# Filler matmuls in TensorE's waits, and a second pass that runs backwards: attention with two FFNs on one core

## The chip, the cores and the metric

The kernel runs on one core of a Trainium2 chip. The metric is the device time of one execution in microseconds (us); lower is better. Engines are named as in the profile: PE is TensorE (its weight loads are PEld), DVE is VectorE, ACT is ScalarE, POOL is GpSimd, SP is SyncE, whose queue issues the DMAs.

## The reference, cut to what matters

```python
batch, n_heads, seq, head_dim = (4, 8, 576, 64)      # q, k, v
n_tokens, d_model = 2304, 512                        # d_ff: 1024, then 2048

def _attn_ref(q, k, v):
    scores = scale * np.matmul(q, k.transpose(0, 1, 3, 2))
    mask = block_i >= block_j                        # blocks of 64 positions
    scores = np.where(mask, scores, -1000000000.0)
    scores = scores - np.max(scores, axis=-1, keepdims=True)
    attn = np.exp(scores)
    attn = attn / (np.sum(attn, axis=-1, keepdims=True) + 1e-09)
    return np.matmul(attn, v)

def _moe_ref(x, w_in, w_out, g_ln):                  # the first FFN
    h = x @ w_in
    e = np.exp(h - np.max(h, axis=-1, keepdims=True))
    solu = h * (e / (np.sum(e, axis=-1, keepdims=True) + 1e-09))
    mu, var = mean and variance of solu over its row
    return ((solu - mu) / np.sqrt(var + 1e-06) * g_ln) @ w_out

def _moe2_ref(x, w_in, w_out):                       # the second FFN
    h = x @ w_in
    return (h * (1.0 / (1.0 + np.exp(-1.702 * h)))) @ w_out
```

All is float32.

## The kernel before, in words

**Three stages share the engines.** Attention runs batch by batch (4 batches, 4 pairs of heads each). For a pair, `scores` multiplies queries by keys on PE, DVE takes the result out of PSUM with the block mask (tile `mask`, zeros but for one corner) and the row maximum (`mx`), ACT makes the exponentials (`P`, `PR`), PE transposes them against `ident` (`u_pt`), and PE multiplies by `v` (`u_pv`). The attention output goes to DRAM (`xd`) and comes back as tiles of 128 tokens (`x`, split into a high and a low part, `xs`) for the first FFN (`h_mm`, `solu_ln`, `ln_t`, `y_mm`). While batch 0 runs, the weights of the first FFN are converted as well (`w1_prep`, tiles `e`, `yo`, `junk`). The first FFN's output goes to DRAM (`y1d`).

**The second FFN** works on chunks of tokens, 640, 640, 512 and 512 of them, and on 8 pairs of weight blocks, `p` = 0 to 7, of which SBUF holds four at a time (`slots`). So it makes two passes over all chunks: pairs 0 to 3 for chunk 0, then chunks 1, 2, 3; then pairs 4 to 7 for chunks 0, 1, 2, 3. A step is one (pair, chunk). In a step `h2_steps` makes seven products (a Strassen-like scheme; tiles `p`, `u`, `hc`, `sg`, then `gH` and `gL`), and `out_steps` adds pair `p`'s part of the output into accumulators that PSUM holds for the chunk, one bank for each 128 tokens. At the end of the first pass over a chunk the accumulators are copied out and stored in DRAM (`part`); at the end of the second pass they are read back (into `land` and `wt`) and added. Before a chunk starts, `y_load` fetches its tokens (`x<-y1d`), `y_sums` makes four sums (tiles `t` and `x`), and `y_split` splits seven operands into high and low parts (tiles `w1i` and `xs`, whose first use is over by then). `prep_w2` makes a pair's weights from DRAM (`wt<-w2d`, then `stmp`, `w2A`, `w2B`, `w2S`, `w2o`), and runs for pairs 4 to 7 while the first pass is at its last chunk.

**The order of instructions** comes from a list scheduler, the class `Recorder`. Every operation is recorded with a priority, and `issue` emits them one by one to the engine on which they can start first, by the costs in `_cost`. Each engine has a time `free[e]` up to which the scheduler believes it busy, and `start` is when it believes the next operation can begin. For some copies and sums it may choose between two engines. PSUM is eight banks that it hands out itself (`bank_free`, `bank_t`). Since every instruction is emitted in `_emit`, all carry line L383 (L387 after the change), and tiles tell them apart. A change of `mode` (the shape of the weights that PE holds) costs 0.09 in the scheduler's account (`SWITCH`), so a matmul put in between can change what is chosen next.

Of the kernel before, what the change touches and what calls it, by code (L numbers as in the profile page):

```python
# [16 lines left out]
ALU = mybir.AluOpType  # L17
# [42 lines left out]
class Recorder:  # L60
# [6 lines left out]
    SPAN = 10  # L67
    OWN = 0.15
    LEAVE = (0, 1, 1)
    SWITCH = 0.09  # L70
    STAY = 0.0
    LOAD = {'vector': 2.0}
# [3 lines left out]
    def __init__(self, tc, banks):  # L76
        self.banks = banks
        self.n_bank = banks.shape[1]
        self.bank_free = [True] * self.n_bank
        self.bank_t = [0.0] * self.n_bank  # L80
        self.n_buf = 0
        self.places = {}

        self.floor = 0.0
        self.tc = tc
        self.nc = tc.nc
        self.prio = 0.0
        self.tag = None
        self.n_tag = {}
        self.open = None  # L90

        self.also = []
        self.ops = []
        self.tensors = {}
        self.free = dict.fromkeys(self.ENGINES, 0.0)
        self.port = 0.0
        self.dma = 0.0
        self.now = 0.0
        self.mode = None
        self.heap = {e: [] for e in self.ENGINES}  # L100
        self.log = []
        for e in self.ENGINES:
            setattr(self, e, _Engine(self, e))
# [281 lines left out]
    def _waiting(self):  # L385
# [5 lines left out]
        ]  # L391
        return min(late, default=1e9)

    def issue(self, tag=None):

        with self.tc.manual_schedule():
            while any(self.heap.values()) and (tag is None or self.n_tag.get(tag, 0)):
                best = None
                waiting = self._waiting()
                for e, heap in self.heap.items():  # L400


                    for prio, i in heap:
                        op = self.ops[i]
                        start = self._start(op, e)
                        if start < 1e9 and prio > waiting + self.YIELD and any(b.at is None for b in op.bufs):
                            start += 1e6
                        key = (start, prio + (self.STAY if self._switch(op, e) else 0.0), i)
# [9 lines left out]
                op = self.ops[i]  # L418
                if start >= 1e6:
                    start = self._start(op, e)  # L420
                for x in op.forms:
                    self.heap[x].remove((prio, i))
                prio = op.prio
                start += self._switch(op, e)
                if e == "tensor":
                    self.mode = op.mode
# [32 lines left out]
                for j in op.users:  # L459
                    o = self.ops[j]  # L460
# [15 lines left out]
def kernel(  # L476
# [19 lines left out]
    NT, DM = out.shape  # L496
# [119 lines left out]

    def clear():
        nc.vector.memset(mask, 0.0)
        nc.vector.memset(mask[0:64, 448:512], -1e30)
        for t in vb:  # L620
            nc.gpsimd.memset(t[64:128, KT - 1], 0.0)
        for x in Pb:
            nc.gpsimd.memset(x["R"][:, S:], 0.0)
        for t in qR:
            for x in t:
                nc.gpsimd.memset(full(x), 0.0)
# [478 lines left out]


    m2_p = ctx.enter_context(tc.tile_pool(name="m2", bufs=1, side="right", reuse_waits="tile"))
    sizes = [640, 640, 512, 512]
    chunks = [(sum(sizes[:i]), n) for i, n in enumerate(sizes)]
    CM = max(sizes)  # L1110
    HM = CM // 2
# [180 lines left out]
    def out_steps(cc, p):  # L1292
        c0, n = chunks[cc]
        g = gs.pop((cc, p))
        O = slots[p % NSLOT][3]
        first, last = p % NSLOT == 0, p % NSLOT == NSLOT - 1
        if first:
            acc[cc] = [nc.bank(0, name="acc") for _ in range(n // 128)]
            for a in acc[cc]:
                a.buf.held = True  # L1300
        if last and p >= NSLOT:
            pb = [pbs[next(n_pb) % len(pbs)] for _ in acc[cc]]
            for i, x in enumerate(pb):
                nc.sync.dma_start(out=x, in_=part[cc][i * 128:(i + 1) * 128])
        for i, a in enumerate(acc[cc]):
            sl = slice(i * 128, (i + 1) * 128)
            todo = [(g[e][x][:, sl], O[e][y], e) for e in range(2) for x, y in ((0, 0), (0, 1), (1, 0))]
            with nc.group():
                for j, (x, y, e) in enumerate(todo):
                    nc.tensor.matmul(a, lhsT=x, rhs=y, start=first and j == 0, stop=last and j == len(todo) - 1)  # L1310
            if last:
                a.buf.held = False

                at = obs + [x[:, 0:DM] for x in tmpb] if p == NPAIR - 1 and cc == len(chunks) - 1 else obs
                o = at[next(n_ob) % len(at)]
                if p < NSLOT:
                    nc.copy(o, a, "av")
                    nc.sync.dma_start(out=part[cc][sl], in_=o)
                else:
                    nc.vector.tensor_tensor(out=o, in0=a, in1=pb[i], op=ALU.add)  # L1320
                    nc.sync.dma_start(out=out[c0 + i * 128:c0 + (i + 1) * 128, :], in_=o)
            yield 6 * 0.231

# [28 lines left out]
    t = f_time  # L1352
# [2 lines left out]
        prep_w2(p)  # L1355
    nc.floor = 0.0
    went_ahead = []
    steps = [(h * NSLOT + p, cc) for h in range(2) for cc in range(len(chunks)) for p in range(NSLOT)]
    for n in range(len(steps) + 1):

        h2 = iter(())
# [7 lines left out]
        while its[0] or its[1]:  # L1369
# [5 lines left out]
                continue  # L1375
            went[i] += cost
            t += cost
        if n < len(steps) and p % NSLOT == NSLOT - 1 and n + 1 < len(steps):
            nc.prio = t + PY
            y_split(steps[n + 1][1])  # L1380
        if NSLOT <= n < NSLOT + 3 * (NPAIR - NSLOT) and n % 2 == 0 and len(went_ahead) < NPAIR - NSLOT:
# [4 lines left out]
        if n + 2 < len(steps) and p % NSLOT == 0:  # L1386

            nx = n + NSLOT
            if nx < len(steps):
                nc.prio = t  # L1390
                y_load(steps[nx][1])
                y_sums(steps[nx][1])
# [42 lines left out]
```

## Time and profile before

| | |
|---|---|
| three timed runs | median 783.81 us (782.36 to 786.83) |
| the profiled execution | 783.7 us |
| its span, first to last instruction | 781.9 us |
| instructions | 13917 |
| PE busy | 762.5 us (98%), 4936 matmuls |
| DVE, ACT, POOL busy | 539.4 us (69%), 442.0 us (57%), 290.8 us (37%) |
| granted TensorE clock, mean | 0.993 |

The busy time of PE has modelled ends, so a busy PE may still be a PE at half clock or with short gaps. What PE waited for, and what clock it was granted, have to be read from their own views. The second FFN begins at about 400 us, its second pass at about 592 us.

### The profile page before, as it was taken

To read this page: it belongs to the slowest core of one execution; us is meant where nothing else is said; L and a number is where in the kernel's file an instruction comes from. 1 tells how busy PE (TensorE), PEld (TensorE's weight loads), DVE (VectorE), ACT (ScalarE), POOL (GpSimd) and SP (SyncE) were. 2 spreads that over 40 slices of the span, in tenths; PEclk is the share of its full clock that TensorE was granted. 3 is DMA by queue.
4 is the path that set the end of the run, shared out by engine and by line. 5 is a ranking of instruction groups with operands and counts; after the bars stand their busy time and mean duration, and the time that the engine had idled before them with its cause. 6 is when DMAs were issued, how large, how long until landed. Compare 5 with 4: busy or idle time off the path is not lost.

```text
span 781.9 us, 13917 instructions
## 1 busy us (share of the span) xinstructions
PE 762.5 (98%) x4936; PEld 652.1 (83%) x4936; DVE 539.4 (69%) x1216; ACT 442.0 (57%) x1005; POOL 290.8 (37%) x365
## 2 busy tenths in 40 slices
PE   7999899999999999999999999999989899999998
PEld 4575586877887888989999998998989799999986
DVE  5978937656564558886748887867899875564644
ACT  6978767676585656565634654535565442433422
POOL 3544540142340264452231533344452253352422
PEclk9999799999999999999999999999999999999999
DMA  8976533442220245446502363455425123050201
GB/s 249 262 242 163 168 105 111 124 137 65 76 70 31 69 151 151 139 143 214 201 30 61 87 220 134 154 162 187 151 74 176 55 74 115 27 162 1 68 15 54
DMA packets 82342, 95.37 MB, mean 122 GB/s; under 512 B 11232, under 2 KB 57952, under 8 KB 82272
## 3 DMA queue, kind: packets, MB, share of 16 engines
q1 hardware_dynamic: 82128, 94.34, 38.6%
q8 instruction: 39, 0.64, 0.3%
q14 instruction: 31, 0.25, 0.1%
q10 hardware_dynamic: 144, 0.13, 0.0%
HBM read 69.21 MB, written 25.24 MB: 121 GB/s over the span
## 4 chain that ended last, share of the span: by engine, by line
PE 89%; DVE 5%; DMA 2%; ACT 1%; issue 1%; POOL 1%; SPq 0%; ACTq 0%; DVEq 0%; POOLq 0%
PE PS L383 89%; DMA xd<-xo 1%; DVE st L383 1%; DMA x<-xd 1%; DVE w2oL L383 1%; DVE t L383 0%; ACT e L383 0%; DMA rawqk<-in_k_dram 0%; ACT P L383 0%; DVE stmp L383 0%; DVE u L383 0%; SPq L383 0%; DVE hc L383 0%; DVE sg L383 0%; DVE w2SL L383 0%
## 5 line engine op out<-in xcount | busy, mean ns | idle before, releaser
L383 ACT ACTIVATE sg<-hc 128x256 f32<-128x256 f32 (+1 forms) x128 | 55.8, 441 | 110.2 <-DVE hc L383 102.7
L383 PE MATMUL PS<-w2oH,gH 128*128 128x512 f32 x288 | 113.0, 392 | 2.4 <-DVE hc L383 2.4
L383 PE MATMUL PS<-w1i,xs 128*128 128x512 f32 x432 | 111.0, 404 | 2.3 <-DVE mx L383 2.3
L383 PE MATMUL PS<-w2oL,gH 128*128 128x512 f32 x288 | 113.0, 392 | 0.0
L383 PE MATMUL PS<-w2oH,gL 128*128 128x512 f32 x288 | 112.0, 389 | 0.0
L383 PE MATMUL PS<-lnTH,w1o 128*128 128x256 f32 x576 | 109.7, 284 | 0.0
L383 PE MATMUL PS<-w1i,w2SH 128*128 128x320 f32 (+1 forms) x512 | 105.2, 296 | 2.1 <-DVE hc L383 2.1
L383 POOL TENSOR_TENSOR sg<-hc,sg 128x256 f32<-128x256 f32 (+1 forms) x53 | 43.8, 827 | 139.4 <-ACT sg L383 137.0
L383 PEld LDWEIGHTS PS<-w1i,xs 128*128 128x128 f32 x432 | 79.5, 192 | 19.2 <-DVE mx L383 3.0
L383 PEld LDWEIGHTS PS<-lnTH,w1o 128*128 128x128 f32 x576 | 90.7, 188 | 1.7 <-issue 1.0
L383 PEld LDWEIGHTS PS<-w1i,w2SH 128*128 128x128 f32 x512 | 84.7, 190 | 5.5 <-DVE hc L383 2.3
L383 DVE CUSTOM_DVE_ANT_0 P<-PS,mask 128x256 f32<-128x256 f32 (+3 forms) x128 | 57.2, 485 | 38.5 <-PE PS L383 36.2
L383 PE MATMUL PS<-lnTL,w1o 128*128 128x256 f32 x288 | 81.3, 282 | 0.0
L383 DVE TENSOR_TENSOR hc<-PS,u 128x320 f32<-128x320 f32 (+1 forms) x96 | 43.4, 455 | 47.4 <-PE PS L383 45.7
L383 PE MATMUL PS<-w1i,w2SL 128*128 128x320 f32 (+1 forms) x256 | 75.8, 296 | 0.0
L383 ACT ACTIVATE P<-P,mx 128x256 f32<-128x256 f32 (+3 forms) x128 | 70.3, 552 | 9.0 <-DVE mx L383 9.0
L383 ACT ACTIVATE gH<-sg 128x320 fp32r<-128x320 f32 (+1 forms) x115 | 50.2, 442 | 39.0 <-DVE sg L383 27.6
L383 PEld LDWEIGHTS PS<-w2oH,gL 128*128 128x128 f32 x288 | 54.1, 188 | 11.9
L383 PEld LDWEIGHTS PS<-w2oH,gH 128*128 128x128 f32 x288 | 54.2, 188 | 11.8 <-DVE hc L383 2.8
L383 PEld LDWEIGHTS PS<-w2oL,gH 128*128 128x128 f32 x288 | 54.2, 188 | 8.3
L383 POOL TENSOR_TENSOR gL<-sg,gH 128x256 fp32r<-128x256 f32 (+1 forms) x47 | 39.7, 851 | 48.0 <-ACT gH L383 44.9
L383 PEld LDWEIGHTS PS<-lnTL,w1o 128*128 128x128 f32 x288 | 54.3, 189 | 0.6 <-DVE lnTL L383 0.2
(191 smaller groups left out, 1667.5 us busy)
## 6 DMA issues: line engine op xcount, KB each, us to landing
land<-in_moe_w_in_dram SPq DMA_DIRECT2D x16, 512.0 KB, 4.5
land<-in_moe_w_out_dram SPq DMA_DIRECT2D x16, 512.0 KB, 3.7
x<-y1d SPq DMA_DIRECT2D x16, 512.0 KB, 6.0
w2d<-wt SPq DMA_DIRECT2D x24, 256.0 KB, 2.1
wt<-w2d SPq DMA_DIRECT2D x24, 256.0 KB, 2.7
y1d<-yo SPq DMA_DIRECT2D x36, 128.0 KB, 1.7
part<-ob SPq DMA_DIRECT2D x18, 256.0 KB, 5.3
e<-in_moe_w_in_dram SPq DMA_DIRECT2D x8, 512.0 KB
```

Of the source, the lines that this page charges most:

```text
L383: getattr(getattr(self.nc, e), name)(*map(real, args), **{k: real(v) for k, v in kw.items()})
```

## The change

It does three things.

1. `_keep_busy` is new. Before `issue` emits an operation on PE, it looks at the time between the end of PE's last work and the start of the next, both in the scheduler's account. While this is over 0.4 (`IDLE`) and the account is below 100 us (`WARM`), it emits matmuls of the zero part of `mask` with itself, 128x128, into a PSUM bank that is free at that time, and counts each as 0.213 (0.427 in the first 4 us). Nothing reads the result. `free["tensor"]` isn't moved by them; only `mode` is set. There are 29 of them in the program.
2. The chunks are 640, 512, 512 and 640 tokens, and the second pass goes through them backwards: 3, 2, 1, 0. Chunk 3 ends the first pass and begins the second, so its five accumulators stay in PSUM over eight pairs (`whole`): no `part` store, no read back, no addition (a copy instead, on ACT or DVE), and no second `y_load`, `y_sums` and `y_split` for it.
3. As the order of the second pass turns, the chunk that ends the program has 640 tokens (five accumulators) instead of 512 (four).

```diff
+    WARM = 100.0
+    IDLE = 0.4
...
+    def _keep_busy(self, mode, start):
+
+        t = max(self.free["tensor"], 0.6)
+        if self.idle is None or t > self.WARM:
+            return
+        if mode != (128, 128):
+            start -= self.SWITCH
+        while start - t > self.IDLE:
+            free = [x for x in range(self.n_bank) if self.bank_free[x] and self.bank_t[x] <= t]
+            if not free:
+                t += 0.05
+                continue
+            x = max(free, key=lambda x: self.bank_t[x])
+            w = self.idle
+            self._emit("tensor", [("matmul", (self.banks[:, x, 0:128],), dict(
+                lhsT=w[:, 0:128], rhs=w[:, 0:128], start=True, stop=True))], lambda a: a)
+            self.mode = (128, 128)
+            self.n_idle += 1
+            t += 0.213 if t > 4.0 else 0.427
+
     def issue(self, tag=None):
...
+                if e == "tensor":
+                    self._keep_busy(op.mode, start)
                 start += self._switch(op, e)
...
         nc.vector.memset(mask, 0.0)
+        nc.idle = mask
...
-    sizes = [640, 640, 512, 512]
+    sizes = [640, 512, 512, 640]
...
-        first, last = p % NSLOT == 0, p % NSLOT == NSLOT - 1
+        whole = cc == len(chunks) - 1
+        first = p == 0 or p == NSLOT and not whole
+        last = p == NPAIR - 1 or p == NSLOT - 1 and not whole
...
-        if last and p >= NSLOT:
+        if last and p >= NSLOT and not whole:
             pb = [pbs[next(n_pb) % len(pbs)] for _ in acc[cc]]
...
-                    nc.vector.tensor_tensor(out=o, in0=a, in1=pb[i], op=ALU.add)
+                    if whole:
+                        nc.copy(o, a, "av")
+                    else:
+                        nc.vector.tensor_tensor(out=o, in0=a, in1=pb[i], op=ALU.add)
...
-    steps = [(h * NSLOT + p, cc) for h in range(2) for cc in range(len(chunks)) for p in range(NSLOT)]
+    steps = [(p, cc) for cc in range(len(chunks)) for p in range(NSLOT)]
+    steps += [(p, cc) for cc in reversed(range(len(chunks))) for p in range(NSLOT, NPAIR)]
...
-        if n < len(steps) and p % NSLOT == NSLOT - 1 and n + 1 < len(steps):
+        if n < len(steps) and p % NSLOT == NSLOT - 1 and n + 1 < len(steps) and steps[n + 1][1] != cc:
             nc.prio = t + PY
             y_split(steps[n + 1][1])
...
-            if nx < len(steps):
+            if nx < len(steps) and steps[nx][1] != cc:
                 nc.prio = t
                 y_load(steps[nx][1])
                 y_sums(steps[nx][1])
```

**Where instructions move, first place: PE at the start of the program.** `rawqk` and `x` are the queries and keys of batch 0's four pairs (`scores`), `ident,P` a transposition. Before:

```order
L383 MATMUL PS<-rawqk_134 128x128 x2
L383 MATMUL PS<-rawqk_134 128x256 x2
L383 MATMUL PS<-rawqk_135 128x128 x2
L383 MATMUL PS<-rawqk_135 128x256 x2
L383 MATMUL PS<-rawqk_136 128x128 x2
L383 MATMUL PS<-rawqk_136 128x256 x2
L383 MATMUL PS<-ident,P_149 128x128
L383 MATMUL PS<-ident,P_151 128x128 x2
L383 MATMUL PS<-x 128x128 x2
```

After:

```order
L387 MATMUL PS<-mask 128x128 x6
L387 MATMUL PS<-rawqk_134 128x128 x2
L387 MATMUL PS<-rawqk_134 128x256 x2
L387 MATMUL PS<-mask 128x128 x4
L387 MATMUL PS<-rawqk_135 128x128 x2
L387 MATMUL PS<-rawqk_135 128x256 x2
L387 MATMUL PS<-mask 128x128 x4
L387 MATMUL PS<-rawqk_136 128x128 x2
L387 MATMUL PS<-rawqk_136 128x256 x2
L387 MATMUL PS<-mask 128x128
L387 MATMUL PS<-ident,P_149 128x128
```

Fifteen mask matmuls stand ahead of the first transposition. The other 14 stand further on in batch 0's attention, in groups of 3, 4, 3, 2 and 2; the last group is in the row before the transposition of `P_158`.

**Second place: PE behind the last group**, from the product with `v` (`pty`) of a pair on. `ident,e` transposes a tile of the first FFN, `w1i,xs` is `h_mm`, `lnTH` and `lnTL` with `w1o` are `y_mm`. Before:

```order
L383 MATMUL PS<-pty_168,v_143 64x64 x2
L383 MATMUL PS<-ident,P_161 128x128 x3
L383 MATMUL PS<-rawqk_134 128x384 x2
L383 MATMUL PS<-ident,P_162 128x128 x3
L383 MATMUL PS<-rawqk_135 128x128 x2
L383 MATMUL PS<-rawqk_135 128x256 x2
L383 MATMUL PS<-w1i,xs 128x512 x6
L383 MATMUL PS<-ident,e_121 128x128 x4
L383 MATMUL PS<-w1i,xs 128x512 x6
```

After:

```order
L387 MATMUL PS<-pty_168,v_143 64x64 x2
L387 MATMUL PS<-ident,e_121 128x128 x8
L387 MATMUL PS<-rawqk_134 128x384 x2
L387 MATMUL PS<-ident,P_161 128x128 x3
L387 MATMUL PS<-ident,P_162 128x128 x3
L387 MATMUL PS<-lnTH,w1o_98 128x256
L387 MATMUL PS<-lnTL,w1o_98 128x256
L387 MATMUL PS<-lnTH,w1o_106 128x256
L387 MATMUL PS<-lnTH,w1o_99 128x256
```

The transpositions of `e_121` and a `y_mm` have come forward, and the scores of `rawqk_135` aren't here any more. All of batch 0's order and of the first FFN's differs in this manner.

**Third place: POOL at the turn from the first pass to the second**, around the preparation of pair 5 (`w2oH_2791`, `w2oL_2797`). Before:

```order
L383 TENSOR_TENSOR gL_2806<-sg_2803,gH_2805 128x256
L383 TENSOR_SCALAR w2oH_2791<-wt_2772 128x512
L383 TENSOR_TENSOR w1i<-t_2795,w1i 128x640
L383 TENSOR_TENSOR w1i<-x,w1i 128x640 x2
L383 TENSOR_TENSOR gL_4092<-sg_2803,gH_4091 128x320
```

After:

```order
L387 TENSOR_TENSOR t_2800<-x 128x512
L387 TENSOR_TENSOR t_2801<-x,t_2800 128x512
L387 TENSOR_TENSOR x<-x 128x2x256
L387 TENSOR_TENSOR sg_2809<-hc_2806,sg_2809 128x320
L387 TENSOR_TENSOR w2oL_2787<-wt_2777,w2oH_2786 128x512
L387 TENSOR_TENSOR gL_4116<-sg_2808,gH_4115 128x320
L387 TENSOR_TENSOR gL_4116<-sg_2809,gH_4115 128x320
L387 TENSOR_TENSOR stmp<-wt_2777,wt_2778 128x256
L387 TENSOR_TENSOR stmp<-wt_2777 128x256
L387 TENSOR_TENSOR gL_2811<-sg_2809,gH_2810 128x320
L387 TENSOR_TENSOR w2oL_2797<-wt_2777,w2oH_2796 128x512
```

The `w1i` rows are `y_split` of the chunk that opened the second pass; there is none at this turn now. Three of the four sums of the next chunk (`t` and `x`), all on DVE at this turn before, are on POOL, and so are two `stmp` and two `w2oL` of the weights.

## Rows read from the trace of the kernel before

**Rows 1.** The page: PE's totals, and the granted clock in 40 slices of the span.

```profile
PE 762.5 (98%) x4936; PEld 652.1 (83%) x4936; DVE 539.4 (69%) x1216; ACT 442.0 (57%) x1005; POOL 290.8 (37%) x365
...
PEclk9999799999999999999999999999999999999999
```

**Rows 2.** Waits of PE, whole span: total us, times, longest.

```profile
PE PS L383 <- DVE hc L383: 4.4, 2, 2.4
PE PS L383 <- DMA rawqk<-in_k_dram: 4.2, 2, 3.7
PE PS L383 <- DVE mx L383: 3.7, 3, 2.3
PE PS L383 <- ACT e L383: 1.8, 1, 1.8
PE PS L383 <- ACT pty L383: 0.8, 2, 0.6
```

**Rows 3.** Timeline of PE and DVE, the turn between passes: start, us, what, [wait before].

```profile
579.31 4.13 POOL L383 TENSOR_TENSOR w1i<-x,w1i 128x640 fp32r<-128x640 f32 x2
...
579.95 4.03 DVE L383 TENSOR_TENSOR w2oL<-wt,w2oH 128x512 fp32r<-128x512 f32 x2
...
585.04 0.56 PE L383 MATMUL PS<-w1i,w2SH 128*128 128x320 f32 x2 [2.07 <-DVE hc L383]
...
604.19 1.50 DVE L383 TENSOR_TENSOR t<-x,t 128x640 f32<-128x640 f32 x1
...
610.02 0.50 PE L383 MATMUL PS<-w2oH,gH 128*128 128x512 f32 x1 [2.36 <-DVE hc L383]
```

**Rows 4.** All instructions of the tile w2oL on DVE: duration ns, min/median/max.

```profile
L383 DVE TENSOR_TENSOR w2oL<-wt,w2oH x15: 677/691/2064, 308.5 to 611.9; 128x512 fp32r<-128x512 f32 x15
```

**Rows 5.** The page's DMA issues: KB each, us to landing.

```profile
part<-ob SPq DMA_DIRECT2D x18, 256.0 KB, 5.3
```

**Rows 6.** Timeline of PE, first 60 us.

```profile
3.71 1.65 PE L383 MATMUL PS<-rawqk 64*128 64x128 f32 x8 [3.71 <-DMA rawqk<-in_k_dram]
5.83 3.30 PE L383 MATMUL PS<-rawqk 64*128 64x128 f32 x16 [0.47 <-DMA rawqk<-in_k_dram]
9.06 0.90 PE L383 MATMUL PS<-ident,P 128*128 128x128 f32 x3
9.89 1.64 PE L383 MATMUL PS<-x 64*128 64x128 f32 x8
11.46 0.55 PE L383 MATMUL PS<-ident,P 128*128 128x128 f32 x3
...
41.05 0.97 PE L383 MATMUL PS<-rawqk 64*128 64x128 f32 x8
...
57.93 2.23 PE L383 MATMUL PS<-ident,P 128*128 128x128 f32 x19
```

**Rows 7.** Timeline of DVE, the two writes of the mask.

```profile
0.93 0.67 DVE L383 MEMSET mask<- 128x512 f32 x2
```

**Rows 8.** Busy time by stretch: PE, PEld, DVE, ACT, POOL, granted clock, DMA share, GB/s.

```profile
11.39:83.07 71.68, 69.14 (x463) 43.55 (x461) 60.40 (x170) 59.46 (x155) 34.45 (x43) 1.00 0.82 242
83.07:93.31 10.24, 7.73 (x25) 5.64 (x26) 10.24 (x22) 6.77 (x19) 8.11 (x9) 0.50 0.31 92
```

**Rows 9.** Timeline of PE, 80 to 98 us.

```profile
82.10 0.91 PE L383 MATMUL PS<-rawqk 64*128 64x384 f32 x2 [1.21 <-DVE mx L383]
83.30 0.90 PE L383 MATMUL PS<-ident,P 128*128 128x128 f32 x3 [0.29 <-ACT P L383]
84.13 1.65 PE L383 MATMUL PS<-rawqk 64*128 64x128 f32 x8
88.06 2.93 PE L383 MATMUL PS<-w1i,xs 128*128 128x512 f32 x6 [2.28 <-DVE mx L383]
...
91.50 2.48 PE L383 MATMUL PS<-w1i,xs 128*128 128x512 f32 x6
...
97.08 1.54 PE L383 MATMUL PS<-w1i,xs 128*128 128x512 f32 x6
```

More of the change, by code (lines that the diff above doesn't have):

```diff
@@ L99, in __init__ @@
         self.mode = None
+        self.idle = None
+        self.n_idle = 0
         self.heap = {e: [] for e in self.ENGINES}
@@ L1312, in out_steps @@
                 a.buf.held = False
-                at = obs + [x[:, 0:DM] for x in tmpb] if p == NPAIR - 1 and cc == len(chunks) - 1 else obs
+                at = obs + [x[:, 0:DM] for x in tmpb] if p == NPAIR - 1 and cc == 0 else obs
                 o = at[next(n_ob) % len(at)]
```

## The prediction

> **What bounds the kernel now.** The page says PE, busy for 762.5 of 781.9 us [rows 1]. Busy time alone proves little here, since the ends of matmuls are modelled, so I went from there to the waits of PE. They confirm it: in the whole span PE stands still for about 15 us (4.4 + 4.2 + 3.7 + 1.8 + 0.8) [rows 2]. The rest of the time is matmuls, whose arithmetic the change doesn't touch. So there are two things to win or lose: PE's waits and PE's clock. [...] Three places matter then: the start, the stretch from 80 to 94 us, and the turn between the second FFN's passes, where the two `hc` waits lie [rows 3]. A measurement of this kernel can tell about 0.5%, 3.9 us, from no change.
>
> **The turn between passes: -4.4 us.** Rows 3 show the first wait being made. POOL works on two `w1i` splits from 579.31 for 4.13 us, DVE on two `w2oL` differences from 579.95 for 4.03 us, and PE waits 2.07 us, up to 585.04, for `hc`, which stands behind them on DVE. A `w2oL` takes 0.69 us in the median [rows 4], so two should take 1.4; they were slow because the two engines got in each other's way. The `w1i` work is `y_split` for chunk 0, which opens the second pass. Now chunk 3 opens it, is already split, and that work is gone. The second wait, 2.36 us up to 610.02, has DVE behind by the four sums for the next chunk (one of them 1.50 us) and a pair's weights. Now the next chunk is smaller, three of its sums are on POOL, and the `y_split` that had put DVE behind is gone. I let both waits go: 2.07 + 2.36 = 4.4. Bounds: 0, if both come back in another form, and 4.4, as PE has no other wait for the second FFN to lose.
>
> **What else leaves the second FFN: 0.** Five `part` stores of 256 KB, five reads back, five additions (now copies), one set of loads, sums and splits. PE waits for none of these outside the turn [rows 2], so they hide beside it. If that cover is missing somewhere, taking them away can only gain. On the queue of SP a part of chunk 2 is now read back soon after it was stored, ahead of the loads of pair 4's weights. A store takes 5.3 us to land [rows 5], so those loads may be late by that much; they are needed a whole chunk later. Five accumulators held through two passes leave three banks for products, as every 640-token chunk does now. At the end PE finishes an accumulator with six matmuls and one output copy and store follow it, in either order of chunks: 0.
>
> **The first fifteen mask matmuls: +1.2 us.** Their price isn't in the trace. The eight rows of a pair's first scores are four matmuls in the program's order, so a float32 matmul runs as two on the chip, and one of 128 columns at full rows is priced best as two transpositions. Nineteen of these take 2.23 us at full clock [rows 6], 0.117 each; so a mask matmul is 0.23 us, and 0.47 at half the clock. The mask is written by 1.60 us (0.93 + 0.67) [rows 7]. Six at half clock then end at 4.4, while the first scores could start at 3.71: +0.7. The next nine cost 4.2 at half clock or 2.1 at full, and only a wait of 0.47 (at 5.83) takes them in [rows 6]. Upper bound, the clock rising no sooner: 0.7 + 4.2 - 0.5 = +4.4. Lower bound, full clock from the first scores on: the scores and transpositions up to 11.5 (1.65 + 3.30 + 0.90 + 1.64 = 7.5) shrink by 0.97/1.65, a gain of 3.1, against 0.7 + 2.1 - 0.5: -0.8. Between them: before, the clock rose at about 11.4, after work that began at 3.71 and had a hole; now work begins 2.1 us earlier, so I let it rise at 9.3. Counting on: scores to 6.0, four masks to 7.9, scores to 9.4, four masks to 10.3, scores to 11.2, one mask, transpositions to 11.8, scores to 12.7, against 11.5 before. I take the round figure +1.2.
>
> **The other fourteen: +1.9 us.** 14 x 0.23 = 3.2 at full clock. In the stretch from 11.39 to 83.07 PE isn't busy for 71.68 - 69.14 = 2.5 us [rows 8], of which 1.21 is the wait up to 82.10, behind the last group. So 1.3 us of the 3.2 falls in time that was idle. Bounds: 0, if DVE and ACT (60.40 and 59.46 of the 71.68 us) set the pace there, and +3.2.
>
> **The stretch from 80 to 94 us: -3.4 us.** PE waited 1.21, 0.29 and 2.28 us there [rows 9], the clock was granted 0.50 from 83.07, and what ran then took 2.93 and 2.48 for six `w1i` matmuls (1.54 at full clock), 1.65 for scores (0.97) and 0.90 for transpositions (0.55) [rows 6, 9]. The clock alone cost 1.39 + 0.94 + 0.68 + 0.35 = 3.4. In the new order eight transpositions and a `y_mm` have moved up to where PE stood, and two scores have left. I expect the waits to stay, as DVE has the same work (10.24 of 10.24 us), and the clock to stay up, as they fall more scattered: -3.4. Bounds: -7.2 with the 3.8 us of waits gone too, and +3.4 for a second fall of the clock in the reordered part.
>
> [...]
>
> **Sum.** 783.7 (the profiled execution: span 781.9 and 1.8 around it) - 4.4 + 1.2 + 1.9 - 3.4 = **779.0 us**. The median of the runs is 783.81, 0.1 from that execution; the forecast is 0.6% below.
>
> **Rivals.**
>
> *The fillers delay PE (slower).* PE works in order, so a filler put where no wait comes holds back the scores behind it, and with them DVE and ACT, which are nearly full up to 83 us. Price: +4.4 for the first fifteen, +3.2 for the others, and the clock falls at 83 as before: 783.7 - 4.4 + 4.4 + 3.2 = 786.9. It decides if the clock rises no sooner than at 11.4. For it: 6.9 us of fillers at half clock against 2.6 us of idle PE. Against: PE is busy without a hole from 1.6 us on. Chance 0.12.
>
> *The clock falls anyway.* Stalls on DVE of the same size come at another place, and the third term is lost: 779.0 + 3.4 = 782.4. For it: the fourteen fillers end before the place where PE waited, and DVE's load is unchanged. Chance 0.14.
>
> *Waits and clock both go.* 779.0 - 3.8 = 775.2. For it: the first FFN's work moved forward fills just these holes. Against: it needs results of DVE itself. Chance 0.16.
>
> *The turn keeps a wait.* POOL now has three sums, two `w2oL` and two `stmp` near one another, beside DVE's own two-input differences, which is the pairing that took 4.03 us for 1.4 [rows 3, 4]. One or both waits come back: 779.0 + 2.1 to 779.0 + 4.4, that is 781.1 to 783.4. Chance 0.12. [...]
>
> **How the numbers follow.** My forecast gets 0.46; its own range is 776.5 to 781.5 by the bounds of its terms. "Faster" means below 779.9: about 0.28 of the forecast's share, all 0.16 of "waits and clock both go", and 0.06 from the forecasts that end lower by a better start or a shorter price of the fillers, and from a single small wait at the turn; together 0.50. "Slower", above 787.7: half of the first rival, and a second fall of the clock on top of the others, 0.10. The rest, 0.40, is within 0.5%. The range from 773.5 to 786.0 leaves out most of the first rival, and below a gain at every place.
>
> **What would show it.** Right: the two `hc` waits between the passes gone from the waits of PE, no `w1i` on POOL at that turn; the first scores of the first pair at about 4.4 us, later ones at the faster pace well before 11 us; the granted clock at 1.00 from 80 to 100 us. Wrong: fillers running while the data of the scores behind them has long landed; a new stretch at 0.50 between 60 and 110 us; an `hc` wait over 1 us near the turn; DVE or ACT late by more than 2 us in the first 80 us.

## The result, and the profile after

The changed kernel takes **773.11 us** (median of four runs, 772.48 to 773.39), the kernel before 785.32 us beside it (782.36 to 787.06): a ratio of 0.9858, 95% interval 0.9829 to 0.9888. It is 1.4% faster. Forecast were 779.0 us and 0.6%; the gain is more than twice that, and the time lies 0.4 us below the low end of the range. The profiled execution took 772.48 us, its span is 770.7, 11.2 us less than before.

PE's totals and its clock in 40 slices, from the page of after; they answer to [rows 1]:

```profile
PE 763.0 (99%) x4994; PEld 655.3 (85%) x4994; DVE 526.6 (68%) x1203; ACT 438.2 (57%) x1001; POOL 288.2 (37%) x359
...
PEclk9999999999999999999999999999999999999999
```

No slice is below 9 tenths. The 58 matmuls more are the 29 fillers, each of which runs as two. The waits of PE over the whole span (total us, times, longest), against [rows 2]:

```profile
PE PS L387 <- DVE mask L387: 1.5, 1, 1.5
PE PS L387 <- POOL xs L387: 0.6, 1, 0.6
PE PS L387 <- DVE mx L387: 0.6, 1, 0.6
PE PS L387 <- DVE pty L387: 0.2, 1, 0.2
```

Both `hc` waits are gone, the `mx` waits have shrunk from 3.7 to 0.6, and the wait of 1.8 for `ACT e`, which the prediction had counted and then not used, is gone too. A wait of 0.6 for `xs` is new; it lies at 536 us, in the second FFN's first pass. Busy time by stretch in after, columns as in [rows 8] (PE, PEld, DVE, ACT, POOL, granted clock, DMA share, GB/s):

```profile
11.39:83.07 71.68, 70.13 (x481) 45.05 (x478) 61.66 (x173) 60.68 (x155) 34.92 (x43) 1.00 0.80 237
83.07:93.31 10.24, 10.24 (x62) 8.55 (x61) 9.65 (x19) 9.83 (x26) 6.52 (x7) 1.00 0.56 167
...
574.00:612.00 38.00, 38.00 (x211) 34.27 (x211) 24.98 (x53) 17.78 (x37) 9.77 (x12) 1.00 0.19 57
```

And the turn between the passes in the kernel before:

```profile
574.00:612.00 38.00, 33.57 (x193) 30.22 (x192) 36.36 (x66) 22.16 (x46) 12.47 (x11) 1.00 0.40 132
```

At the turn PE is busy for all of the 38 us, 4.4 more than before, and DVE has 11 us less to do. In the 10.24 us from 83.07 on PE had 25 recorded matmuls at 0.50 [rows 8]; now it has 62 at 1.00. How much was won before the second FFN is read from its first product with `w2oH` in PE's timeline, before and then after:

```profile
406.94 0.39 PE L383 MATMUL PS<-w2oH,gH 128*128 128x512 f32 x1
```

```profile
399.43 0.39 PE L387 MATMUL PS<-w2oH,gH 128*128 128x512 f32 x1
```

So 7.5 of the 11.2 us were won ahead of it, in attention and the first FFN, and 3.7 in the second FFN. The start of the program, PE's timeline in after, against [rows 6]:

```profile
1.47 2.93 PE L387 MATMUL PS<-mask 128*128 128x128 f32 x12 [1.47 <-DVE mask L387]
4.33 0.99 PE L387 MATMUL PS<-rawqk 64*128 64x128 f32 x8
5.25 1.16 PE L387 MATMUL PS<-mask 128*128 128x128 f32 x8
...
9.46 0.82 PE L387 MATMUL PS<-ident,P 128*128 128x128 f32 x6
10.21 0.93 PE L387 MATMUL PS<-x 64*128 64x128 f32 x8
```

The first scores take 0.99 us where they took 1.65, the time of eight such matmuls in the stretch at 0.50 too [rows 9]: by these times the clock was up as soon as the first fillers were done. Its record begins at 4.50 us, at 1.00; before, at 11.39. Scores of four pairs and six transpositions end at 11.14; before, the same work ended at 12.01.

### The profile page after: what moved, and what is told of

Same layout as the page of the kernel before. It is cut to its first block, busy times and chain, and to the rows that moved or that the text cites. A ratio compares the mean times of both kernels' runs of the same rounds, so it can differ in the third digit from the quotient of the medians.

```text
span 770.7 us, 14020 instructions
## 1 busy us (share of the span) xinstructions
PE 763.0 (99%) x4994; PEld 655.3 (85%) x4994; DVE 526.6 (68%) x1203; ACT 438.2 (57%) x1001; POOL 288.2 (37%) x359
## 4 chain that ended last, share of the span: by engine, by line
PE 94%; ACT 1%; DMA 1%; DVE 1%; POOL 1%; issue 1%; SPq 0%; ACTq 0%; DVEq 0%
PE PS L387 94%; DMA land<-in_moe_w_out_dram 1%; ACT P L387 1%; DMA e<-in_moe_w_out_dram 0%; DVE w1o L387 0%; POOL xs L387 0%; POOL yo L387 0%; POOL e L387 0%; ACT e L387 0%; ACT pty L387 0%; POOL sg L387 0%; DVE e L387 0%; DVE ob L387 0%; DVE wt L387 0%; ACT wt L387 0%
## 5 line engine op out<-in xcount | busy, mean ns | idle before, releaser
L387 ACT ACTIVATE sg<-hc 128x320 f32<-128x320 f32 (+1 forms) x128 | 56.5, 442 | 108.4 <-DVE hc L387 94.3
L387 PE MATMUL PS<-w1i,xs 128*128 128x512 f32 x432 | 108.4, 399 | 0.0
L387 POOL TENSOR_TENSOR sg<-hc,sg 128x256 f32<-128x256 f32 (+1 forms) x54 | 46.1, 854 | 128.8 <-ACT sg L387 128.7
L387 DVE CUSTOM_DVE_ANT_0 P<-PS,mask 128x512 f32<-128x512 f32 (+3 forms) x128 | 57.1, 485 | 30.9 <-PE PS L387 30.6
L387 POOL TENSOR_TENSOR gL<-sg,gH 128x256 fp32r<-128x256 f32 (+1 forms) x44 | 36.6, 838 | 52.1 <-ACT gH L387 51.3
L387 DVE TENSOR_TENSOR gL<-sg,gH 128x320 fp32r<-128x320 f32 (+1 forms) x84 | 47.8, 574 | 11.5 <-ACT gH L387 9.8
```

The source lines that it names most:

```text
L387: getattr(getattr(self.nc, e), name)(*map(real, args), **{k: real(v) for k, v in kw.items()})
```

## The experiments

Ratios are to runs of the kernel before on the same chip (medians 784.97 to 785.77 us). "Order" means the order of the real instructions up to the second FFN; "turn" is the second pass in reverse with its five accumulators kept.

### Which part brings it: fillers, order or turn

**Fillers and order, without the turn.** The second FFN is that of the kernel before, all else is changed.

```diff
-    sizes = [640, 512, 512, 640]
+    sizes = [640, 640, 512, 512]
...
-    steps = [(p, cc) for cc in range(len(chunks)) for p in range(NSLOT)]
-    steps += [(p, cc) for cc in reversed(range(len(chunks))) for p in range(NSLOT, NPAIR)]
+    steps = [(h * NSLOT + p, cc) for h in range(2) for cc in range(len(chunks)) for p in range(NSLOT)]
```

> The 29 fillers alone; the second FFN as in the kernel before (chunks 640, 640, 512, 512, second pass forwards). Theory A (the two halves of the change don't touch each other): the lead over the kernel before that the changed kernel has when the second FFN begins, about 7.5 us, stays and nothing is added: 777 to 778.5 us against 785, and both hc waits of about 2 us stand at the turn. Rival: the turn's waits depend on the order before them and go here too, 773 to 775.

Measured: 781.1 us, 0.9945 [0.9928, 0.9962], above both ranges. Up to the second FFN the run was 6.7 us ahead of the kernel before; at its end only 1.2 us. The lead was lost at the turn.

**The turn alone.** No fillers; the order up to the second FFN is that of the kernel before.

```diff
         nc.vector.memset(mask, 0.0)
-        nc.idle = mask
```

> The second FFN's new chunks and backward second pass alone, no fillers; up to the second FFN the order is that of the kernel before. Theory A: the two hc waits go (4.4 us) and a new wait of up to 1 us appears in the first pass: 3.5 to 4.5 us below the kernel before, so about 781. Rival: the clean turn needed the earlier start or other order of the changed kernel: 783.5 to 785.

Measured: 779.82 us, 0.9937 [0.9913, 0.9961]. No `hc` wait is left at the turn. The `mx` waits (4.5 us in two, the longest 3.2) and the clock's fall near 85 us (0.50 from 85.33 to 92.15) stay.

**The changed order, no filler emitted.** The scheduler still notes the weight shape that a filler would leave behind, so that every real instruction stands where the changed kernel has it.

```diff
-            w = self.idle
-            self._emit("tensor", [("matmul", (self.banks[:, x, 0:128],), dict(
-                lhsT=w[:, 0:128], rhs=w[:, 0:128], start=True, stop=True))], lambda a: a)
             self.mode = (128, 128)
```

> The changed kernel with its order of all real instructions, but none of the 29 fillers. Theory B (the fillers keep the clock up; the order by itself is worth little): the clock is low up to about 11 us again and falls again somewhere between 70 and 95 us: 777 to 781 us. Rival C (the new order takes the stalls at 80 to 94 us away by itself, and the later fillers only cost): 771 to 775, with the clock at 1.00 from 12 us on.

Measured: **771.74 us**, 0.9835 [0.9804, 0.9865], rival C: no slower than with the fillers. Its waits of PE:

```profile
PE PS L387 <- DMA rawqk<-in_k_dram: 4.4, 3, 3.7
PE PS L387 <- DVE mx L387: 1.0, 2, 0.6
PE PS L387 <- DVE e L387: 0.9, 1, 0.9
```

and its clock from the end of the start on:

```profile
12.53:770.00 757.47, 750.20 (x4898) 644.13 (x4896) 523.41 (x1176) 432.24 (x982) 284.78 (x342) 1.00 0.38 117
```

The record of the clock begins only at 12.53 us here, 8 us later than in after, and the clock then didn't fall before the end: this run kept it up without fillers. The same order doesn't always; a later run of it without fillers, with the old second FFN, shows a fall at 77.93 us.

**The fillers in the old order.** They are emitted, and the scheduler doesn't note them.

```diff
                 lhsT=w[:, 0:128], rhs=w[:, 0:128], start=True, stop=True))], lambda a: a)
-            self.mode = (128, 128)
             self.n_idle += 1
```

> Fillers are emitted but leave no trace in the scheduler's state, so all real instructions stand in the order of e2 (and up to the second FFN in that of the kernel before), with 27 fillers between them: 15 ahead of the first transposition, and 7 where the kernel before stood still from 82 to 88 us. Theory B: the clock is up from about 4.5 us and doesn't fall at 83: 4 to 6 us below e2, about 775 to 777. Rival C: the stalls on DVE stay and so does the fall, or is only shortened: within 2 us of e2, 779 to 783.

Measured: 780.74 us, 0.9942 [0.9924, 0.9961], rival C; without the fillers the same order took 0.9937. The clock still fell, to 0.50 from 87.60 to 91.01 us.

**The changed order with the old second FFN, no fillers**: the second FFN of the first experiment, and no filler emitted as in the third.

> The changed kernel's new order up to the second FFN, no filler emitted, and the second FFN of the kernel before. It fills the fourth corner of the table (order or not, turn or not). Theory T (the lead of the new order and the gain of the turn add up): the turned kernel with the old order gained 5.9 us on the shared time of before, so this one is slower than the new order alone with its turn (771.7) by that, 777.6 us (776.5 to 778.7), with the same two hc waits of about 2 us at the turn and no fall of the clock. Theory U (the old second FFN loses part of the lead again when it comes out of the new order, as the run with fillers did, where PE waited for w1i and hc and the clock fell at 605 us): 780.5 us (779.5 to 782), PE waiting 5 us or more between 560 and 620 us.

Measured: 780.6 us, 0.9943 [0.9918, 0.9967], as theory U has it. PE's waits, and then two stretches at the lower clock:

```profile
PE PS L387 <- DVE w1i L387: 2.9, 1, 2.9
PE PS L387 <- DVE hc L387: 2.6, 1, 2.6
```

```profile
77.93:81.34 3.41, 3.41 (x12) 1.45 (x12) 3.37 (x8) 2.56 (x6) 1.26 (x2) 0.50 0.72 274
607.00:610.41 3.41, 3.41 (x10) 2.84 (x11) 2.86 (x7) 2.51 (x6) 1.10 (x2) 0.50 0.25 73
```

Now the table is full:

| | old second FFN | turned |
|---|---|---|
| old order, no fillers | 1 | 0.9937 |
| old order, fillers | not run | 0.9942 |
| new order, no fillers | 0.9943 | 0.9835 |
| new order, fillers | 0.9945 | 0.9858 |

In each of the three pairs the fillers as work make no measurable difference. Order and turn gain some 0.6% each when alone, and 1.65% together: they aren't independent. Coming out of the new order, the old `y_split` is late by 2.92 us at 577.36, and what `y_split` costs at the turn is more than the 4.4 us that it cost from the old order. The turned second FFN has none there.

**Only the first 15 fillers emitted**, in the changed order.

```diff
-            self._emit("tensor", [("matmul", (self.banks[:, x, 0:128],), dict(
+            if self.n_idle < 15:
+                self._emit("tensor", [("matmul", (self.banks[:, x, 0:128],), dict(
...
```

> The changed kernel with the first 15 mask matmuls only; the other 14 are counted by the scheduler but not emitted, so the real instructions keep the new order. Without any filler this order took 771.7, with all 29 773.1. Theory H (the head earns its keep, since the clock is at its upper level from 4.5 us instead of 12.5; the later fourteen cost): 770.4 us (769.5 to 771.3), first scores late by about 0.6 us but everything from 12 us on ahead of the order alone. Theory N (head neutral: what the clock gives the fillers take, and the later ones cost their time): 771.7 (771.3 to 772.3). Theory L (the head costs its 1.2 to 1.4 us, the later fourteen lie in idle time): 773.0 (772.5 to 773.6).

Measured: 771.89 us, 0.9825 [0.9800, 0.9850], theory N: the first fifteen neither gain nor cost, and the other fourteen cost 1.2 us by the medians (773.11 with all), 0.6 by the profiled spans (770.7 against 770.1). The intervals of the two ratios overlap. Here the first scores ran at the lower clock although the same twelve records stood ahead of them:

```profile
1.47 2.93 PE L387 MATMUL PS<-mask 128*128 128x128 f32 x12 [1.47 <-DVE mask L387]
4.33 1.65 PE L387 MATMUL PS<-rawqk 64*128 64x128 f32 x8
```

so the head's lead differs from run to run. Nor does it last: the row of 24 `w1i,xs` records in PE's timeline begins at 87.14 us with the order alone and at 86.89 with all fillers, 0.25 us apart; the rest of what the earlier clock gave is gone by then.

### What in the order it is

**Another price for a change of shape**, no fillers, turned: a third order.

```diff
-    SWITCH = 0.09
+    SWITCH = 0.13
```

> No fillers and no record of any; the turned second FFN; only the scheduler's price of a change of weight shape is 0.13 instead of 0.09, which gives a third order, different from both. Theory D (the order before was an unlucky draw around 83 us, most others have no fall of the clock there): 773.5 us (771 to 776), no stretch at 0.50 between 60 and 110 us. Theory E (the changed kernel's order is the lucky one: the stall with its fall of the clock comes in most orders, since DVE is full there): 780 us (777 to 784), a stretch at 0.50 between 60 and 110 us and a wait for mx or P of over 1.5 us.

Measured: 774.47 us, 0.9860 [0.9831, 0.9890]. The time is theory D's, the view theory E's: PE waited 2.70 us for `mx` up to 75.42, and the clock was at 0.50 from 74.64 to 81.46. Neither theory had the mechanism. DVE had idled for a result of POOL and then converted weights ahead of the `mx` that PE needed; DVE's row:

```profile
73.03 0.69 DVE L387 SCALAR_TENSOR_TENSOR e<-e 128x512 int32<-128x512 int32 x1 [1.37 <-POOL e L387]
```

**Only the later fillers noted**, none emitted, turned: a fourth order.

```diff
-            self.mode = (128, 128)
+            if t > 15.0:
+                self.mode = (128, 128)
```

> No filler emitted; the turned second FFN; the scheduler takes the weight shape for changed only at fillers counted later than 15 us in its account, not at the first fifteen. A fourth order. If the order that helps hangs on the later bookkeeping, at the place where PE stood behind the last group: 771.7 us (770.5 to 773), no stretch at 0.50 near 85 us. If it hangs on the head's: 779.8 us (778 to 781.5), as with the old order, the stretch at 0.50 near 85 us and mx waits of 3 us. A time outside both would say that each order is a draw of its own.

Measured: 778.67 us, 0.9909 [0.9876, 0.9943]; PE waits 5.0 us for `mx`, 2.62 of them up to 88.45, and the clock is at 0.50 from 84.10 to 94.30. The fall returns when the head's notes are missing: without them all four engines run the old order up to 106 us, so that in the stretch this is the old order once more and not a fourth.

What holds PE up near 85 us in the old order? The old order in the run of the turn alone, DVE and then POOL in the timeline (start, us, what):

```profile
83.52 0.69 DVE L387 TENSOR_TENSOR xs<-x,xs 128x512 fp32r<-128x512 f32 x1
84.13 2.64 DVE L387 TENSOR_TENSOR st<-st 128x1 f32<-128x1 f32 x1
86.69 0.68 DVE L387 CUSTOM_DVE_ANT_0 P<-PS,mask 128x512 f32<-128x512 f32 x1
```

```profile
84.28 1.26 POOL L387 TENSOR_TENSOR x<-x,r 128x512 f32<-128x512 f32 x1
85.52 0.65 POOL L387 TENSOR_SCALAR e<-e 128x512 f32<-128x512 f32 x1
86.12 0.63 POOL L387 TENSOR_SCALAR yo<-e 128x512 f32<-128x512 f32 x1
```

`st<-st` multiplies one column by another, for the first FFN's normalization. It ends when POOL's row of three ends, and behind it on DVE stand the mask and maximum (`P`, `mx`) for which PE waits 3.21 us:

```profile
88.95 2.92 PE L387 MATMUL PS<-w1i,xs 128*128 128x512 f32 x6 [3.21 <-DVE mx L387]
```

All instructions of this form, ns min/median/max, in the kernel before and in after:

```profile
L383 DVE TENSOR_TENSOR st<-st x14: 156/488/2654, 62.9 to 376.4; 128x1 f32<-128x1 f32 x14
```

```profile
L387 DVE TENSOR_TENSOR st<-st x14: 145/174/1243, 59.9 to 356.8; 128x1 f32<-128x1 f32 x14
```

The longest is 2654 before, and 2642, 2649 and 2653 in the three other runs with the stretch at 0.50 near 85 us (turn alone, fillers in the old order, later notes); all four have the old order there. The third order's wait up to 75.42 is of another kind: its longest such product took 1.25 us. In after, the additions `x<-x,r` fell to DVE itself (1.34 us for two, from 81.09), so that POOL has no such row there. The scheduler counts 0.10 us for this product and, since its operands have one column, leaves it out of `port`, by which its account puts certain longer operations of DVE and those of POOL one after the other.

**POOL's three instructions left out**, old order, turned.

```diff
-                self._emit(e, calls, real)
+                if e == "gpsimd":
+                    self.n_pool = getattr(self, "n_pool", 0) + 1
+                if not (e == "gpsimd" and self.n_pool in (54, 55, 56)):
+                    self._emit(e, calls, real)
```

> The old order with the turned second FFN and no fillers (779.8 us), but three instructions of POOL near 84 us are left out (the addition of x and r for one tile of tokens, and two copies of a weight block's conversion, 1.26, 0.65 and 0.63 us). In the run of this order DVE's product of two columns, st from st, began at 84.13 and took 2.64 us, just as long as POOL worked through these three; a product of that kind takes 0.15 us elsewhere, the scheduler counts 0.10. Theory K (POOL's run holds DVE, DVE is then late with mx, PE waits 3.2 us and its clock falls): the product takes under 0.8 us, the longest mx wait is under 1.2 us, and the time 775.5 us (774 to 777.5), lower in the range if the clock no longer falls near 85 us. Theory F (DVE is full there whatever POOL does): 779.8 us (778.8 to 780.8), the same wait at another instruction.

Measured: 775.29 us, 0.9871 [0.9848, 0.9894], theory K. The two products took 193 and 528 ns, the longest `mx` wait was 0.9 us, and the clock didn't fall (1.00 from 80 to 100 us):

```profile
84.55 1.66 PE L387 MATMUL PS<-w1i,xs 128*128 128x512 f32 x6 [0.92 <-DVE mx L387]
```

Not all of the profiled lead is the edit's. PE is 2.0 us ahead of the run of the turn alone at the transposition before the place of the three (82.23 against 84.20); near 71 us POOL, and DVE behind it, had waited less for a weight block's DMA (0.82 us against 1.89). At the third row of six `w1i,xs` it is 5.9 ahead (88.24 against 94.09). So some 3.9 us are won in the stretch, the clock included; the medians differ by 4.5.

**The products moved to POOL**, old order, turned, nothing left out.

```diff
-                self._emit(e, calls, real)
+                name, args, kw = calls[0]
+                small = e == "vector" and name == "tensor_tensor" and kw["out"].shape[-1] == 1
+                self._emit("gpsimd" if small else e, calls, real)
```

> The old order with the turned second FFN and no fillers (779.8 us); all products of two columns (st from st) that the scheduler gave to DVE are issued on POOL instead, at the same place of the order, the account unchanged. Nothing is left out. Theory K (DVE loses its time in these products beside POOL): DVE goes straight on, the mx wait of 3.2 us is under 1.2 us, 776 us (774 to 778). Theory F (no gain, or the stall moves to the next instruction of DVE that reads two tiles of SBUF): 779.8 us (778.8 to 781).

Measured: **773.12 us**, 0.9856 [0.9828, 0.9884]: below the range of theory K, and as fast as the changed kernel, from the old order and without a filler. POOL's timeline, and PE's where 3.21 us of wait stood:

```profile
81.58 0.54 POOL L387 TENSOR_TENSOR st<-st 128x1 f32<-128x1 f32 x1
82.09 0.23 POOL L387 TENSOR_SCALAR qRH<-qkH 64x64 fp32r<-64x64 f32 x1
82.29 1.27 POOL L387 TENSOR_TENSOR x<-x,r 128x512 f32<-128x512 f32 x1
83.53 0.18 POOL L387 TENSOR_TENSOR st<-st 128x1 f32<-128x1 f32 x1
```

```profile
83.82 1.65 PE L387 MATMUL PS<-w1i,xs 128*128 128x512 f32 x6 [0.36 <-DVE mx L387]
```

DVE's product no longer stands in front of the mask. By the same two places PE goes from 2.1 us ahead of the turn alone (82.06 against 84.20) to 6.5 (87.64 against 94.09): 4.3 us are won in the stretch, the clock included. At the second FFN it is 9.2 ahead, with a shorter `ACT e` wait (0.90 us against 1.87) and no fall of the clock near 297 (1.00 as the mean of the run). The medians differ by 6.7; the profiled execution of the turn alone (781.83) was among its slowest.

**The same move in the new order**, no fillers.

> The same move of the products of two columns from DVE to POOL, in the new order without fillers (771.7 us), where DVE's product took at most 0.65 us up to 100 us and 1.24 us later. Theory K (what is left to gain is what these products still lose, and DVE isn't on the path after 100 us): 771.2 us (770.2 to 772.0). Theory F (the products now wait behind POOL's longer work, and what needs them on ACT is late): 773 us (772.2 to 775).

Measured: 774.03 us, 0.9855 [0.9836, 0.9874], theory F: no gain, and by its median 2.3 us more than the order alone (1.2 by the profiled spans). PE waits where it hadn't:

```profile
84.25 1.09 PE L387 MATMUL PS<-ident,e 128*128 128x128 f32 x8 [1.28 <-ACT e L387]
```

In this order no such product had taken more than 0.65 us up to 100 us, so DVE had little to get back; on POOL what needs them comes later.

**The reverse: work for nothing on POOL** beside the product, new order, no fillers.

```diff
+                if e == "vector" and name == "tensor_tensor" and kw["out"].shape[-1] == 1 and 78 < start < 90:
+                    if not self.n_dummy:
+                        for _ in range(6):
+                            self._emit("gpsimd", [("tensor_tensor", (), dict(
+                                out=self.scratch, in0=self.idle[:, 0:176], in1=self.idle[:, 176:352], op=ALU.add))], lambda a: a)
...
```

(`scores` also asks for six PSUM buffers here, of which it uses two as before; the order up to the second FFN, but for the six, is that of the order alone.)

> The reverse: the new order without fillers (771.7 us), with six additions of 128x176 to a scratch tile put on POOL just ahead of DVE's product of two columns at 81 us; some 2.5 us of work for nothing on an engine that is idle for 0.7 us there. Theory K: the product takes 2 to 3 us again instead of 0.4, PE waits 1.5 to 2.5 us more for mx or P between 82 and 90 us, and the time is 774.5 us (773.2 to 778, the upper part if the clock falls again). Theory F: PE has enough else to do there, 771.7 us (771.2 to 772.5).

Measured: 774.05 us, 0.9862 [0.9838, 0.9885]. The time is theory K's, the path only in part. DVE, then POOL:

```profile
80.60 0.91 DVE L388 TENSOR_TENSOR st<-st 128x1 f32<-128x1 f32 x2
81.43 2.02 DVE L388 TENSOR_TENSOR x<-x,r 128x512 f32<-128x512 f32 x2
```

```profile
80.75 4.39 POOL L388 TENSOR_TENSOR scratch<-mask 128x176 f32<-128x176 f32 x6
```

The two products took 0.91 instead of 0.38, the two additions 2.02 instead of 1.34, and POOL's six 4.39 instead of an estimated 2.6 (by the 1.27 that an addition of 512 columns takes on POOL): side by side both engines took longer. No wait of 1.5 us for `mx` came, and the clock stayed up (1.00 from 80 to 100 us). The profiled span grew by 1.4 us (771.7 against 770.3): the row `w1i,xs` that begins at 87.14 with the order alone begins at 87.58, and the other 0.9 us are lost later, up to the second FFN (401.00 against 399.63), by a path that stays open.

## Why the prediction was right, and where its steps failed

"Faster" was right, with a chance of 0.50; the time is 5.9 us below the forecast, just outside the range, and the gain is 1.4% where 0.6% was forecast. The turn alone would have carried the direction (0.9937).

**The turn, -4.4: right, by its mechanism and its size.** PE's busy time from 574 to 612 us rose by 4.4 (33.57 to 38.00), no `w1i` stands on POOL there up to 611.66, and the longest `w2oL` on DVE fell from 2064 ns [rows 4] to 1366. "What else leaves: 0" held up to the 0.6 us of the `xs` wait. What the term didn't say is that its worth depends on the order ahead of it: 0.6% from the old order, and 1.1% from the new one (0.9943 to 0.9835).

**The first fifteen, +1.2: wrong in sign.** I let the clock rise at 9.3 us; in after it was up from 4.5, and the work up to the sixth transposition was done 0.9 us earlier. That the rise comes earlier by just as much as PE begins earlier was my estimate, and no run shows it: in after PE began 2.2 us earlier (1.47 against 3.71) and the record of the clock 6.9. The half clock at the start is a reading of durations: scores took 1.65 us there, as at 0.50, and 0.97 later [rows 6, 9]. The lower bound of the term, full clock from the first scores on, is what this run had; the run with the first 15 alone lay between the bounds (the same work done at 12.12, 0.1 later than before). Without fillers the new order ended that work at 12.38.

**The other fourteen, +1.9: mis-sized.** They cost 0.6 us by the profiled spans (770.7 against 770.1 with the first 15 alone) and 1.2 by the medians. Those at 69.8 and 73.5 us stand in waits that the order alone has too: 0.92 us for `e` there became 0.20 behind six records of the mask, and 0.53 for `pty` became 0.22. All 29 together are worth -0.2 us up to the second FFN (399.43 against 399.63 with the order alone) and +0.4 in the span (770.7 against 770.3), +1.4 by the medians, where I had +3.1.

**The stretch from 80 to 94 us, -3.4: the step whose mechanism failed.** That the clock stays up when waits fall more scattered was an estimate of mine, which no run shows; in after the waits of 1.21, 0.29 and 2.28 us went, and it was granted 1.00 from 80 to 100 us. "I expect the waits to stay, as DVE has the same work" took DVE's 10.24 busy us in 10.24 [rows 8] for work. Some 2.5 us of it were waiting: a product of one column, which takes 0.16 at the least, stands for 2.65 and counts as busy. DVE in the kernel before:

```profile
83.23 2.65 DVE L383 TENSOR_TENSOR st<-st 128x1 f32<-128x1 f32 x1
```

DVE's own timeline there, which I had read at the turn alone, has the price in sight. The rival "waits and clock both go" is what happened, and its reason, that first-FFN work fills the holes, is not shown to be it: the runs show that POOL's row beside the product made the hole of 2.28 us. The hole of 1.21 before it is another: at 75.59 DVE had idled 1.30 us for POOL's `e`, which had waited for a weight block's DMA, and in the run with three instructions left out, which changes nothing before 82 us, both waits are gone. The waits and the clock together are worth 7.2 us [rows 9]; the whole lead at the second FFN is 7.5, of which 1.8 is the `ACT e` wait at 296 us [rows 2], which no term of mine touched, and about 0.2 the fillers. That leaves 5.5: the new order gives back some 1.7 us elsewhere. With the order alone PE is idle for 2.63 us between 60 and 83.07 us, in the kernel before for 1.90, of which 1.21 is the wait up to 82.10; so some 1.9 us of new waits lie there.

The `ACT e` wait goes back to the same clash. In the kernel before, two products of one column, of 0.16 us each at the least, took 2.48 us beside two of POOL's instructions; ACT's `e` started as they ended, and PE's wait ended with it, at 296.42. DVE, then POOL:

```profile
292.55 2.48 DVE L383 TENSOR_TENSOR st<-st 128x1 f32<-128x1 f32 x2 [0.68 <-POOL st L383]
```

```profile
292.48 1.30 POOL L383 TENSOR_TENSOR xs<-x,xs 128x512 fp32r<-128x512 f32 x1
293.74 1.28 POOL L383 TENSOR_TENSOR x<-x,r 128x512 f32<-128x512 f32 x1
```

With the products on POOL, in the same order, the wait was 0.90 us. These two weren't moved by themselves.

Sum, by the profile: -0.2 (fillers) -5.5 (order, up to 100 us) -1.8 (`ACT e`) +0.6 (`xs`) -4.4 (turn) = -11.3, against -11.2 in the span. The 5.5 is what the other figures leave of 7.5, so only the second FFN's part checks itself (-3.8 against -3.7). Against the forecast's -4.7 the fillers are off by 3.3, the stretch by 2.1 and the `ACT e` wait by 1.8: the two filler terms missed by the most, the stretch by its mechanism.

**The change doesn't act as its text says.** The fillers were to fill waits and hold the clock. Emitted without being noted they gain nothing that the times show; noted without being emitted they bring the whole gain up to the second FFN (399.63 against 399.43), by making the scheduler choose differently. The prediction put the gain down to the order, not to the fillers, and that was right. It gave the order no cause that could be tested.

One column was enough for the clash: in the run of the turn alone the first of the two products took 2.64 us beside 2.54 of POOL (1.26 + 0.65 + 0.63), and with POOL's three left out the two took 193 and 528 ns.

What stays open: why the new order alone, in the old second FFN, is late with `y_split` by 2.92 us, which wasn't tried apart; and how common the clash is, since near 85 us one order alone, the old one, was shown to have it.

## What to carry to other kernels

An engine that shows as full in the bottleneck's stretch has to be read instruction by instruction: the one whose duration was many times its form's minimum (2654 ns, 156 at the least) was a wait here, and the other engine's timeline beside it named the cause, which runs that moved or removed either side then showed. Moving fourteen products of one column to the engine that held them up (773.12 us) gave as much as the reordering by fillers; in an order without that clash the same move cost 2.3 us by the medians, so it is made where the clash is, and not as a rule. And where an edit passes through a list scheduler, the edit's work and its effect on the order have to be run apart before either is credited: here 7.3 of the 7.5 us gained up to the second FFN came with the order alone, and one number of the scheduler (0.13 for 0.09) moved the time by 5.3 us too, against the turn alone. The fastest kernels of the study are the order without fillers (771.74 us) and with the first 15 (771.89).

## What the runs showed of the hardware

In these runs the granted clock didn't follow from the length of a wait. Before and in the run of the turn alone, the same transposition waited for the same result (PE's timeline):

```profile
296.42 1.09 PE L383 MATMUL PS<-ident,e 128*128 128x128 f32 x8 [1.79 <-ACT e L383]
```

```profile
296.39 1.47 PE L387 MATMUL PS<-ident,e 128*128 128x128 f32 x8 [1.87 <-ACT e L387]
```

In the first the clock stayed at 1.00, in the second it was at 0.50 from 296.96 on:

```profile
296.96:300.37 3.41, 3.41 (x12) 2.83 (x11) 2.55 (x5) 2.16 (x4) 0.00 (x0) 0.50 0.22 60
```

It fell at 77.93 in a run whose longest wait shortly before was 1.33 us, for `e` (new order, old second FFN), and not at all in one with a wait of 1.3 us for `e` as well and a further one of 1.28, up to 84.25 (the products on POOL, new order; 1.00 from 11.39 to 100 us). Nor was the start the same from run to run: after the same twelve mask records the first scores took 0.99 us in after and 1.65 in the run with the first 15 alone; and without fillers, in the same order, PE had 36 records and 7.02 busy us up to 11.39 us in one run (the order alone), and 42 and 7.05 in another (with the old second FFN).
